# A spectral filter mixed with a Mish MLP: idle matmuls on a built-in constant, and the second piece of w1 loaded in two

## The chip, the cores and the metric

One core of one Trainium2 chip runs the whole program. The metric is the device time of one execution in microseconds, the median over several runs. The core's engines are TensorE (matmuls and transposes into PSUM), VectorE, ScalarE, GpSimd and SyncE; each works through its own queue in order, and semaphores connect them. Transfers between HBM and SBUF are issued by SyncE (SP), ScalarE or GpSimd and are carried by 16 DMA engines.

## The reference

With S = 2048 rows, D = 512 columns and F = 1792 hidden columns, all in bfloat16:

```python
def reference(A_x, A_w_r, A_w_i, B_x, B_w1, B_b1, B_w2, gate_w):
    x = A_x
    g = sigmoid((x * gate_w).sum(-1, keepdims=True))
    X = rfft2(x.astype(float32), axes=(-2, -1)) * (A_w_r + 1j * A_w_i)
    a = irfft2(X, s=(S, D), axes=(-2, -1)).astype(bfloat16)
    h = einsum("bsd,df->bsf", x, B_w1) + B_b1
    b = einsum("bsf,fd->bsd", h * tanh(softplus(h)), B_w2)
    return g * a + (1 - g) * b
```

The two branches share x. Branch a is a two-dimensional Fourier filter; branch b is a two-layer network with the Mish activation.

## The kernel before

The 2048 rows are 16 tiles of 128 rows, handled as four chunks of four tiles. The layouts keep the contraction on the 128 partitions, so each x tile is first transposed on TensorE (L516) and copied to `xT`.

Branch b: layer 1 is one group of four matmuls of 512 columns for each chunk and each of 14 hidden tiles (L575, tasks `mm1_c_ft`), Mish with the bias on ScalarE (L560), and layer 2 for each row tile (L903, the last tile in L886). For chunk 0 the first four hidden tiles are computed earlier and in finer steps, while x and w1 arrive: the tasks `early0` to `early3` take one 128-row slice of w1 each for the first half of chunk 0, and `late0` to `late3` one hidden tile each for the second half (all L590, 256 columns).

Branch a: both Fourier transforms are products with constant tables. The row transform is done per tile (`a1_t`, L609 to L612, with the table `FD`) on sums and differences of transposed tiles that VectorE forms (L541). The column transform takes two stages with a round trip through DRAM between them; the filter follows, and the inverse goes the same way back (L745 to L846). At the end the two branches are mixed and stored.

Nothing of the order is written by hand. Every piece of work is a task with an engine, a modelled duration, what it reads and writes, and a priority. `_Graph.schedule` plays the tasks through a simple model of the five engines and one DMA pipe, and the order in which it starts them becomes the order of each engine's queue. A transfer lasts its bytes divided by a rate `bw` in this model. `bw` is a number of the model alone: it changes the order in which tasks stand, never the transfer.

The head of the program, which the change touches:

- SP issues its transfers in the order in which they are written down: `ld_x00` (x tiles 0 and 2), `ld_w1d0`, `ld_x01` (tiles 1 and 3), `ld_w1d1` to `ld_w1d3` (the rest of w1's first 512 columns), `ld_w1_4` (hidden tiles 4 to 7), `ld_fd` (the table FD), `ld_x10` (chunk 1 of x), `ld_w1_8`, `ld_m1`, then the rest. `ld_b1` is issued by ScalarE. GpSimd's eight loads of the filter and two of w2 wait for `ld_w1_8`.
- VectorE fills `zt` with zeros (task `zero`, L500). ScalarE runs one Mish of one element from it (task `table`, L501), which loads the activation table.
- TensorE multiplies `zt` with itself (tasks `warm0` to `warm59`, L504) into PSUM bank 6, whose content is overwritten later. These idle matmuls are fillers: the planner takes them whenever TensorE has nothing better, and drops all that are left once `early0` has started. Of the 60, 14 remain in the program, all of 256 columns.
- `tr_small` (L519) transposes the bias; the eight transposes of x tiles 0 and 2, then of 1 and 3, are the tasks `tr0d0` to `tr1d3` (L516), and VectorE and ScalarE copy them to `xT` in turn (L529).

The lines of the idle matmuls:

```python
G.add("zero", "dve", 0.15, lambda e: e.memset(zt[:, :], 0.0), writes=["zt"], prio=99.0)
for i in range(NWARM):
    n_ = 256 if i < 15 else 128
    G.add(f"warm{i}", "pe", n_ / 1200, lambda e, n_=n_: e.matmul(ps[:, 6, 0:n_], zt[:, 0:128], zt[:, 0:n_], start=True, stop=True),
       reads=["zt"], prio=1.0).filler = True
```

Of the kernel before, what the change touches and what calls it, by code (L numbers as in the profile page):

```python
# [7 lines left out]
BF = mybir.dt.bfloat16  # L8
F32 = mybir.dt.float32
AF = mybir.ActivationFunctionType  # L10
# [305 lines left out]
def _build(nc, A_x, A_w_r, A_w_i, B_x, B_w1, B_b1, B_w2, gate_w, out):  # L316
# [9 lines left out]
    G = _Graph()  # L326
    es = ExitStack()
    with es:
        def sb(name, shape, dt):
            return es.enter_context(nc.sbuf_tensor(name, shape, dt))  # L330

        xo = sb("xo", [128, NT, 512], BF)
# [4 lines left out]
        act = sb("act", [128, 3, NFT, 512], BF)  # L337
        w1_sb = sb("w1_sb", [128, 4, F], BF)
# [8 lines left out]
        Ybuf = sb("Ybuf", [128, 32 * KR], BF)  # L347
        junk = sb("junk", [128, 512], BF)
        gwb = sb("gwb", [128, 512], BF)
        zt = sb("zt", [128, 256], BF)  # L350
        braw = sb("braw", [14, 128], BF)
        b1f = sb("b1f", [128, NFT], F32)
        gdot = sb("gdot", [128, NT], F32)
# [12 lines left out]
        q1 = sb("q1", [128, 2, 2, 16], F32)  # L366
# [25 lines left out]
        ps = es.enter_context(nc.psum_tensor("ps", [128, 8, 512], F32))  # L392
        psb = ps.bitcast(BF)

        xv = A_x[0].rearrange("(s p b) d -> p s b d", s=2, b=8)
        ov = out[0].rearrange("(s p b) d -> p s b d", s=2, b=8)
        w1v = B_w1.rearrange("(dt p) f -> p dt f", p=128)
# [7 lines left out]
        def new_sem(name):  # L405
            return es.enter_context(nc.semaphore(name))
# [5 lines left out]
        def dma(name, dst, src, reads=(), writes=(), nbytes=0, deps=(), is_out=False, prio=None, queue="sp", bw=300e3):  # L412
            dur = 1.0 if queue == "pool" else 0.5

            def fn(e, _dst=dst, _src=src):
                return e.dma_start(_dst, _src)

            t = G.add(name, queue, dur, fn, reads=reads, writes=writes, lat=2.0 + nbytes / bw, deps=deps, prio=prio)
            t.xfer = nbytes / bw
            t.isdma = True  # L420
            if is_out:
                t.sem = out_sem
                n_out_dma[0] += 1
                t.semval = 16 * n_out_dma[0]
            else:
                t.sem = new_sem("d_" + name)
                t.semval = 16
            return t
# [16 lines left out]
        def evict(name, n, dst, src, reads, writes, prio=None, rate=1.0):  # L445
# [9 lines left out]
              reads=["ones"], writes=["perm"])  # L455
        G.add("id14", "pool", 0.2, lambda e: e.affine_select(out=id14[:, :], in_=id14[:, :], pattern=[[1, 14]],
                                                             compare_op=ALU.is_equal, fill=0.0, base=0, channel_multiplier=-1),
              reads=["ones"], writes=["id14"])

        def ld_x(c, s0, s1):  # L460
            dma(f"ld_x{c}{s0}", xo[:, 4 * c + 2 * s0:4 * c + 2 * s1, :].rearrange("p (s b) d -> p s b d", b=2), xv[:, s0:s1, 2 * c:2 * c + 2, :],
                writes=[("x", t) for t in range(4 * c + 2 * s0, 4 * c + 2 * s1)], nbytes=128 * 2048 * (s1 - s0), bw=330e3 if c == 1 else 380e3)

        def ld_x0(b):
            dma(f"ld_x0{b}", xo[:, b:4:2, :], xv[:, :, b, :], writes=[("x", b), ("x", 2 + b)], nbytes=128 * 2048, bw=(218e3, 350e3)[b])

        def ld_w1d(dt_):
            dma(f"ld_w1d{dt_}", w1_sb[:, dt_, 0:512], w1v[:, dt_, 0:512], writes=[("w1d", dt_)], nbytes=128 * 1024, bw=350e3)

        def ld_w1(lo, hi):  # L470
            return dma(f"ld_w1_{lo}", w1_sb[:, :, 128 * lo:128 * hi], w1v[:, :, 128 * lo:128 * hi],
                       writes=[("w1", f) for f in range(lo, hi)], nbytes=512 * 256 * (hi - lo), bw=220e3 if lo == 4 else 380e3)

        dma("ld_b1", braw[:, :], B_b1.rearrange("(ft p) -> ft p", p=128), writes=["braw"], nbytes=3584, queue="act", prio=100.0)
        ld_x0(0)
# [1 line left out]
        ld_x0(1)  # L477
        for dt_ in range(1, 4):
            ld_w1d(dt_)
        ld_w1(4, 8)  # L480
        dma("ld_fd", FDs[:], d_FD[:], writes=["FD"], nbytes=128 * 1536, bw=262e3)
        ld_x(1, 0, 2)
        t_w1 = ld_w1(8, 14)
        dma("ld_m1", m1g1[:, 0:2048], d_M1.rearrange("p b h c m -> p (b h c m)"), writes=["m1"], nbytes=128 * 4096)
        ld_x(2, 0, 2)
# [4 lines left out]
        for i in range(2):  # L490
            for q in (0, 2, 1, 3):
                dma(f"ld_W{i}{q}", WT[32 * q:32 * q + 32, i, :, :].rearrange("p g k -> p (g k)"), Wv[i][q],
                    writes=[("W", i, q)], nbytes=32 * 8224, queue="pool", deps=[t_w1])
        WALL = [("W", i, q) for i in range(2) for q in range(4)]
        for h in range(2):
            dma(f"ld_w2_{h}", w2_sb[:, 7 * h:7 * (h + 1), :], w2v[:, 7 * h:7 * (h + 1), :],
                writes=[("w2", h)], nbytes=128 * 7 * 1024, queue="pool", deps=[t_w1])


        G.add("zero", "dve", 0.15, lambda e: e.memset(zt[:, :], 0.0), writes=["zt"], prio=99.0)  # L500
        G.add("table", "act", 1.5, lambda e: e.activation(q1[:, 0, 0, 0:1], zt[:, 0:1], AF.Mish), reads=["zt"], prio=99.0)  # L501
        for i in range(NWARM):
            n_ = 256 if i < 15 else 128
            G.add(f"warm{i}", "pe", n_ / 1200, lambda e, n_=n_: e.matmul(ps[:, 6, 0:n_], zt[:, 0:128], zt[:, 0:n_], start=True, stop=True),  # L504
               reads=["zt"], prio=1.0).filler = True


        SP0 = PR['sp0']
# [2 lines left out]
        def f_tr(e, ts, dts, at):  # L511
# [8 lines left out]
           reads=["braw", "id14"], writes=[("bank", 0)], prio=SP0 + 4.0)  # L520
        G.add("ev_small", "act", 0.25, lambda e: e.activation(b1f[:, :], psb[:, 0, 0:14], AF.Copy), reads=[("bank", 0)], writes=["b1f"], prio=SP0 + 1.05)
        for b in range(2):
            for dt_ in range(4):
                bk = (dt_ + 1) % 4
                pe(f"tr{b}d{dt_}", 2 * mm((256, 128)[b]), lambda e, dt_=dt_, bk=bk, b=b: f_tr(e, (b, 2 + b), (dt_,), lambda t, d_: (bk, t // 2)),
                   reads=[("x", b), ("x", 2 + b), "perm"], writes=[("bank", bk)], prio=SP0 + 1.0 + 2.5 * b - 0.01 * dt_)
# [3 lines left out]
                      reads=[("bank", bk)], writes=[("xT", t, dt_) for t in (b, 2 + b)], prio=SP0 + 1.1)  # L530

        for c in range(NCH):
            for t in range(4 * c, 4 * c + 4):
                if c > 0:
                    pe(f"tr{t}", 4 * mm(128), lambda e, t=t: f_tr(e, (t,), range(4), lambda t, dt_: (1, dt_)), reads=[("x", t), "perm"],
                       writes=[("bank", 1)], prio=SP0 + 1.0)
# [7 lines left out]
            for h, op in ((0, ALU.add), (1, ALU.subtract)):  # L544
# [3 lines left out]
                lo, hi = uv[:, 0:2, r2, :], uv[:, 2:4, r2, :]  # L548
# [45 lines left out]
        for dt_ in range(4):  # L594
            t_e = pe(f"early{dt_}", 4 * mm(256) * (1.8 if dt_ == 0 else 1), lambda e, dt_=dt_: f_early(e, range(4), (dt_,), 0), writes=[("bank", b) for b in EB],
                     reads=[("xT", 0, dt_), ("xT", 2, dt_), ("w1d", dt_)], prio=PR['mm1c0'] + 8)
            if dt_ == 0:
                G.filled = t_e
        for ft in range(4):
            pe(f"late{ft}", 4 * mm(256), lambda e, ft=ft: f_early(e, (ft,), range(4), 1), writes=[("bank", EB[ft])],  # L600
               reads=[("xT", t, dt_) for t in (1, 3) for dt_ in range(4)] + [("w1d", dt_) for dt_ in range(4)], prio=PR['mm1c0'] + 7 - 0.01 * ft)
            mish(0, ft, EB[ft])

        for t in range(NT):
            a1b = t % 2 if t >= 8 else 0

            def f_a1(e, t=t, a1b=a1b):
# [9 lines left out]
               writes=[("bank", a1b)], prio=SP0)  # L617
# [4 lines left out]
            if t % 4 == 3:  # L622
# [17 lines left out]
                for h in range(2):  # L640
                    t_r1w.append(dma(f"r1w{t}_{h}", scr1_w[h][:, b0:b0 + 8, :], Y1[64 * h:64 * h + 64, b0:b0 + 8, :],
                                     reads=[("Y1", b0 + i) for i in range(8)], writes=[("scr1", b0 + i, h) for i in range(8)],
                                     nbytes=64 * 8 * 512, prio=SP0 + 1.0, bw=180e3))
# [3 lines left out]
        for t in range(NT):  # L647
            G.add(f"gdot{t}", "dve", dve_dur(512) + 0.1,
                  lambda e, t=t: e.scalar_tensor_tensor(out=junk[:, :], in0=xo[:, t, :], scalar=1.0, in1=gwb[:, :],  # L649
                                                        op0=ALU.mult, op1=ALU.mult, accum_out=gdot[:, t:t + 1]),  # L650
                  reads=[("x", t), "gw"], writes=[("gd", t), "junk"], deps=s1_tasks[2:3])
# [37 lines left out]
        for n in range(4):  # L689
            t_r1r.append(dma(f"r1r{n}", In2[:, :, 2 * n:2 * n + 2, :].rearrange("p q u k -> p q (u k)"), scr1_r[:, :, 512 * n:512 * n + 512],  # L690
                             reads=[("scr1", b, h) for b in range(32) for h in range(2)],
                             writes=[("In2", q, u) for q in range(4) for u in (2 * n, 2 * n + 1)],
# [43 lines left out]
        for n in range(4):  # L736
            zb = n % 2

            def f_s2(e, n=n):
                ins = None  # L740
                for c in range(2):
                    for q in range(4):
                        for h in range(2):
# [6 lines left out]
                               reads=[("In2", q, 2 * n + uu) for q in range(4) for uu in range(2)] + ["sm"], writes=BSB))  # L750
            for i in range(4):
                h, uu = divmod(i, 2)
                u, pb = 2 * (2 * n + uu) + h, uu
                for (nm, Pb, Wu) in (("1", P1b, WT[:, :, u, 0:256]), ("2", P2b, WT[:, ::-1, u, 0:256])):
# [5 lines left out]
                          reads=[("bank", 2 * h), ("bank", 2 * h + 1)] + WALL, writes=[("P" + nm, pb)])  # L760
                for (c, nm, Pb, op) in ((0, "1", P1b, ALU.subtract), (1, "2", P2b, ALU.add)):
# [3 lines left out]
                                reads=[("P" + nm, pb)], writes=[("Z", zb, i, c)])  # L765
                if n == 0 and i == 1:
                    s2_tasks.append(pe("s2x", 0.8, f_s2x, reads=[("In2", q, u_) for q in range(4) for u_ in range(8)] + ["sm", "rr"],
                                       writes=[("bank", 0), ("bank", 1)]))
# [4 lines left out]
                          reads=["q"], writes=["zr"])  # L773
                    G.add("zi", "pool", 0.15, lambda e: e.tensor_tensor(out=zi[:], in0=q2[:, 0], in1=q2[:, 1], op=ALU.add),
                          reads=["q"], writes=["zi"])
                    G.add("z0r", "pool", 0.15, lambda e: e.tensor_tensor(out=z0[:, 0, :], in0=zr[:, 0, :], in1=zi[:, 1, :], op=ALU.subtract),
                          reads=["zr", "zi"], writes=["z0r"])
                    G.add("z0i", "pool", 0.15, lambda e: e.tensor_tensor(out=z0[:, 1, :], in0=zi[:, 0, :], in1=zr[:, 1, :], op=ALU.add),
                          reads=["zr", "zi"], writes=["z0i"])
            if n == 0:  # L780
                G.add("gexp", "pool", 2.9, lambda e: e.tensor_tensor(out=gexp[:, :], in0=gbase[:, :], in1=gdot[:, :], op=ALU.pow),  # L781
                      reads=[("gd", t) for t in range(NT)] + ["gbase"], writes=["gexp"])
                G.add("gden", "pool", 0.2, lambda e: e.tensor_scalar(out=gexp[:, :], in0=gexp[:, :], scalar1=1.0, scalar2=None, op0=ALU.add),
                      reads=["gexp"], writes=["gden"])
                G.add("gcol", "dve", 0.2, lambda e: e.reciprocal(out=gcol[:, :], in_=gexp[:, :]), reads=["gden"], writes=["gcol"])
                G.add("omg", "dve", 0.1, lambda e: e.tensor_scalar(out=omg[:, :], in0=gcol[:, :], scalar1=-1.0, scalar2=1.0, op0=ALU.mult, op1=ALU.add),
                      reads=["gcol"], writes=["omg"])
            G.add(f"wc_{n}", "pool", 0.2, lambda e, n=n, zb=zb: e.tensor_copy(
                out=Zb[:, zb, :, :, :, 0], in_=z0[:].rearrange("p c (u h) -> p h c u", h=2)[:, :, :, 2 * n:2 * n + 2]),
                reads=["z0r", "z0i"], writes=[("Z", zb, 4)])  # L790

            def f_s2i(e, zb=zb):
# [10 lines left out]
               writes=BSB)  # L803
# [3 lines left out]
            for h in range(2):  # L807
                t_r2w.append(dma(f"r2w{n}{h}", scr2_w[h][:, :, 512 * n:512 * n + 512],
                                 T2s[64 * h:64 * h + 64, :, 2 * n:2 * n + 2, :].rearrange("p q u k -> p q (u k)"),
                                 reads=[("T2s", n, 0), ("T2s", n, 1)], writes=[("scr2", n, h)], nbytes=64 * 4096))  # L810
# [3 lines left out]
        for tq in range(8):  # L814
            b0 = 4 * tq
            dma(f"r2r{tq}", T2r[:, b0:b0 + 4, :], scr2_r[:, b0:b0 + 4, :],
                reads=[("scr2", n, h) for n in range(4) for h in range(2)], writes=[("T2r", b0 + i) for i in range(4)],
# [49 lines left out]
        for c in range(NCH):  # L867
# [7 lines left out]
            for tl in range(4):  # L875
                t = 4 * c + tl
                bank = 4 + (t % 2)
                if t == NT - 1:
                    G.cur_prio = PR['mm2'] - 10
                    for i, (c0, w_) in enumerate(((0, 384), (384, 128))):  # L880
                        cs_, bk = slice(c0, c0 + w_), 1 + i

                        def f_mm2h(e, t=t, tl=tl, bk=bk, hb=hb, cs_=cs_, w_=w_):
                            ins = None
                            for ft in range(NFT):
# [5 lines left out]
                           writes=[("bank", bk)])  # L891
                        G.add(f"fin_{t}_{i}", "dve", dve_dur(w_, True),
                              lambda e, t=t, bk=bk, cs_=cs_, w_=w_: e.scalar_tensor_tensor(out=xo[:, t, cs_], in0=ps[:, bk, 0:w_], scalar=omg[:, t:t + 1],
                                                                                    in1=ga[:, t, cs_], op0=ALU.mult, op1=ALU.add),
                              reads=[("bank", bk), "omg", ("ga", t, 0), ("ga", t, 1), ("x", t)], writes=[("o", t, i)], prio=PR['fin'])
# [3 lines left out]
                for lo, hi in ((0, 4), (4, 7), (7, 11), (11, 14)):  # L899
                    def f_mm2(e, t=t, tl=tl, bank=bank, lo=lo, hi=hi, hb=hb):  # L900
# [7 lines left out]
                       reads=[("act", hb, ft) for ft in range(lo, hi)] + [("w2", lo // 7)], writes=[("bank", bank)])  # L908
                if t < NBF:
                    evict_b(t, bank)  # L910
                else:
                    G.add(f"fin_{t}", "dve", dve_dur(512, True),
                          lambda e, t=t, bank=bank: e.scalar_tensor_tensor(out=xo[:, t, :], in0=ps[:, bank, :], scalar=omg[:, t:t + 1],
                                                                           in1=ga[:, t, :], op0=ALU.mult, op1=ALU.add),
                          reads=[("bank", bank), "omg", ("ga", t, 0), ("ga", t, 1)], writes=[("x", t), ("o", t)], prio=PR['fin'])
# [116 lines left out]
```

## Time and profile before

| what | value |
|---|---|
| time, median of 3 runs (lowest, highest) | 135.4 us (135.06, 135.48) |
| the profiled execution, its time and its span | 135.63 us, 133.9 us |
| TensorE busy | 128.9 us |
| VectorE, ScalarE, GpSimd busy | 88.9, 79.6, 27.4 us |
| HBM read and written | 14.35 MB, 6.29 MB |
| `ld_x00`: issued at, to landing | 0.80 us, 2.7 us |
| `ld_w1d0`: issued at, to landing | 1.31 us, 3.4 us |
| `ld_w1_4`: issued at, to landing | 3.74 us, 5.8 us |
| `ld_fd`: issued at, to landing | 4.21 us, 5.8 us |

The span runs from the first to the last recorded instruction; the time of an execution is 1.7 us longer than its span. "Busy" is the union of an engine's recorded instructions. Matmuls overlap in their pipeline and their ends are modelled, so for TensorE the step from one start to the next tells more than the length of one.

### The profile page before, as it was taken

The numbers are of one execution on the slowest core, as the hardware profiler recorded it, in microseconds if no ns is written. First come the engines' busy times: TensorE is split into PE (matmuls) and PEld (weight loads), VectorE is DVE, ScalarE is ACT, GpSimd is POOL, SyncE is SP. The second block draws the span as 40 slices with busy tenths as digits, with TensorE's granted clock in tenths as the row PEclk, the third lists the DMA queues.
The fourth block names the chain that finished last, engine by engine and source line by source line (L and its number), as shares of the span: only waits on it lengthen the run. The fifth ranks groups of instructions, "written<-read, shape, count | busy, mean of one in ns | idle before, by whom it ended". The sixth has DMA issues, their size and how long they took to land.

```text
span 133.9 us, 2695 instructions
## 1 busy us (share of the span) xinstructions
PE 128.9 (96%) x1030; PEld 69.5 (52%) x1047; DVE 88.9 (66%) x213; ACT 79.6 (59%) x130; POOL 27.4 (20%) x56
## 2 busy tenths in 40 slices
PE   6999999999999999999999999999999999999992
PEld 4885655655544443443443443443445877755452
DVE  0286298989689982963893893794001699999422
ACT  4258798899988786605256657434333789792000
POOL 2000793014000009583440440440000000000000
PEclk9999999999999999999999999999999999999999
DMA  3899999999262399450600600600649700305321
GB/s 114 238 294 367 397 284 299 288 366 344 62 157 58 99 293 334 98 220 0 157 5 0 157 2 0 156 6 0 157 150 277 204 2 0 130 32 215 113 102 42
DMA packets 18937, 20.82 MB, mean 155 GB/s; under 512 B 1196, under 2 KB 16172, under 8 KB 18540
## 3 DMA queue, kind: packets, MB, share of 16 engines
q1 hardware_dynamic: 17888, 16.67, 41.1%
q0 software_dynamic: 864, 3.94, 9.4%
q8 instruction: 8, 0.13, 0.4%
q10 hardware_dynamic: 172, 0.04, 0.1%
q14 instruction: 5, 0.04, 0.1%
HBM read 14.35 MB, written 6.29 MB: 154 GB/s over the span
## 4 chain that ended last, share of the span: by engine, by line
PE 90%; ACT 6%; issue 1%; DVE 0%
PE ps L903 34%; PE ps L575 31%; PE ps L846 5%; ACT act L560 3%; PE ps L828 3%; ACT Ybuf L447 3%; PE ps L504 2%; PE ps L516 2%; PE ps L886 2%; PE ps L612 2%; PE ps L590 2%; PE ps L798 2%; PE ps L745 2%; PE ps L630 1%; PE ps L609 1%
## 5 line engine op out<-in xcount | busy, mean ns | idle before, releaser
L575 PE MATMUL ps<-xT,w_sb 128*128 128x512 bf16 x199 | 48.1, 379 | 0.8 <-issue 0.2
L903 PE MATMUL ps<-w_sb,act 128*128 128x512 bf16 x202 | 46.9, 379 | 0.6 <-issue 0.3
L560 ACT ACTIVATE act<-ps,b1f 128x512 bf16<-128x512 f32 x56 | 37.8, 692 | 12.8 <-PE ps L575 10.9
L903 PEld LDWEIGHTS ps<-w_sb,act 128*128 128x128 bf16 x210 | 20.2, 98 | 23.2 <-issue 1.2
L575 PEld LDWEIGHTS ps<-xT,w_sb 128*128 128x128 bf16 x208 | 19.4, 98 | 22.3 <-issue 2.1
L756 DVE TENSOR_TENSOR misc<-ps,WT 128x512 f32<-128x512 f32 x32 | 19.8, 681 | 5.9 <-PE ps L745 5.9
L858 ACT ACTIVATE xo<-ps,omg 128x512 bf16<-128x512 f32 x12 | 8.3, 690 | 19.5 <-PE ps L903 18.9
L762 POOL TENSOR_TENSOR misc<-misc 128x255 bf16<-128x255 f32 x17 | 12.1, 732 | 18.4 <-DVE misc L756 18.4
L446 DVE CAST Ybuf<-ps 128x512 bf16<-128x512 f32 (+1 forms) x9 | 8.2, 926 | 9.1 <-PE ps L798 7.3
L850 ACT ACTIVATE misc<-ps,gcol 128x512 f32<-128x512 f32 x16 | 10.7, 692 | 2.5 <-PE ps L846 2.4
L853 DVE TENSOR_TENSOR Tg<-misc 128x256 bf16<-128x256 f32 x32 | 11.7, 419 | 0.6 <-ACT misc L850 0.5
L446 DVE CAST misc<-ps 128x512 bf16<-128x512 f32 x7 | 4.8, 687 | 10.5 <-PE ps L828 10.5
L447 ACT ACTIVATE Ybuf<-ps 128x512 bf16<-128x512 f32 (+1 forms) x15 | 9.9, 714 | 2.9 <-PE ps L798 2.8
L649 DVE SCALAR_TENSOR_TENSOR junk<-xo,gwb 128x512 bf16<-128x512 bf16 x16 | 11.0, 690 | 0.7
L846 PE MATMUL ps<-GDs,misc 128*128 128x256 bf16 x64 | 9.3, 273 | 0.0
L447 ACT ACTIVATE Abuf<-ps 128x512 bf16<-128x512 f32 x13 | 7.7, 604 | 0.0
L446 DVE COPY xT<-ps 128x512 bf16<-128x512 bf16 x10 | 4.2, 422 | 4.6 <-PE ps L516 4.5
L516 PEld LDWEIGHTS ps<-pid,xo 128*128 128x128 bf16 x64 | 5.6, 111 | 3.1 <-DVE xT L446 0.4
L846 PEld LDWEIGHTS ps<-GDs,misc 128*128 128x128 bf16 x64 | 6.0, 98 | 2.1
L516 PE MATMUL ps<-pid,xo 128*128 128x128 bf16 x64 | 6.8, 243 | 0.0
L781 POOL TENSOR_TENSOR gexp<-gbase,gdot 128x16 f32<-128x16 f32 x1 | 2.9, 2943 | 18.5 <-DVE junk L649 18.5
L612 PE MATMUL ps<-FDs,Tg 128*128 128x256 bf16 x32 | 6.0, 273 | 0.0
(85 smaller groups left out, 112.8 us busy)
## 6 DMA issues: line engine op xcount, KB each, us to landing
scr<-Ybuf SPq DMA_DIRECT2D x16, 256.0 KB, 3.9
Abuf<-scr SPq DMA_DIRECT2D x4, 512.0 KB, 5.8
Abuf<-scr SPq DMA_DIRECT2D x8, 256.0 KB, 4.9
w_sb<-in_B_w_dram POOLq DMA_DIRECT2D x2, 896.0 KB, 14.2
out_dram<-xo SPq DMA_DIRECT2D x7, 256.0 KB, 2.1
xo<-in_A_x_dram SPq DMA_DIRECT2D x3, 512.0 KB, 9.8
WT<-in_A_w_r_dram POOLq DMA_DIRECT2D x4, 257.0 KB, 9.1
WT<-in_A_w_i_dram POOLq DMA_DIRECT2D x4, 257.0 KB, 10.8
```

Of the source, the lines that this page charges most:

```text
L446: G.add_multi(name, [("dve", dve_dur(n, rate=rate), lambda e: e.tensor_copy(out=dst, in_=src)), ("act", act_dur(n), lambda e: e.activation ...
L447: ("act", act_dur(n), lambda e: e.activation(dst, src, AF.Copy))],
L516: ins = e.transpose(psb[:, bank, 128 * col:128 * col + 128], xo[:, t, 128 * dt_:128 * (dt_ + 1)], perm[:, :])
L560: lambda e: e.activation(act[:, c % 3, ft, :].rearrange("p (t a b) -> p t a b", t=4, b=4), ps[:, bank, :].rearrange("p (t b a) -> p t a b" ...
L575: ins = e.matmul(ps[:, bank, :], w1_sb[:, dt_, 128 * ft:128 * (ft + 1)], xT[:, dt_, 4 * c:4 * c + 4, :], start=(dt_ == 0), stop=(dt_ == 3))
L649: lambda e, t=t: e.scalar_tensor_tensor(out=junk[:, :], in0=xo[:, t, :], scalar=1.0, in1=gwb[:, :], op0=ALU.mult, op1=ALU.mult, accum_out= ...
L756: lambda e, Pb=Pb, Wu=Wu, h=h, uu=uu, pb=pb: e.tensor_tensor(out=Pb[:, pb, :].rearrange("p (c j m) -> p c j m", c=2, j=2), in0=ps[:, 2 * h ...
L762: fz = (lambda e, c=c, Pb=Pb, op=op, pb=pb, h=h, uu=uu, zb=zb: e.tensor_tensor(out=Zb[:, zb, h, c, uu, 1:256], in0=Pb[:, pb, 1:256], in1=P ...
L846: ins = e.matmul(ps[:, yk, 256 * (j // 2):256 * (j // 2) + 256], TT[:, ts_, j // 2, s1, j % 2, :], GDs[:, j, :], start=(j % 2 == 0), stop= ...
L850: G.add(f"geo_{t}", "act", act_dur(512, True), lambda e: e.activation(gEO[:, gb, :], ps[:, yk, :], AF.Copy, scale=gcol[:, t:t + 1]), reads ...
L853: fg = (lambda e, i=i, op=op: e.tensor_tensor(out=ga[:, t, 256 * i:256 * i + 256], in0=gEO[:, gb, 0:256], in1=gEO[:, gb, 256:512], op=op))
L903: ins = e.matmul(ps[:, bank, :], act[:, hb, ft, 128 * tl:128 * (tl + 1)], w2_sb[:, ft, :], start=(ft == 0), stop=(ft == NFT - 1))
```

## The change

It does four things.

1. The tile `zt` and its zero fill go. The idle matmuls and the one-element Mish read the program's built-in constant 1.0, which is filled before the engines are released. It is one float32 number on each partition, read again and again with a step of zero. Neither waits for anything.
2. Of the idle matmuls only the first 8 have 256 columns, the others 128. The planner now keeps 17: 8 of 256 and 4 of 128 ahead of `tr_small`, 5 of 128 behind it, all ahead of the first transposes of x.
3. `ld_w1_4` is split into `ld_w1_4` (hidden tiles 4 and 5) and `ld_w1_6` (6 and 7), with `ld_fd` between them.
4. The rates of several loads in the planner's model are set anew.

```diff
-            dma(..., bw=330e3 if c == 1 else 380e3)                    # ld_x
+            dma(..., bw=308e3 if c == 1 else 380e3)
-            dma(f"ld_x0{b}", ..., bw=(218e3, 350e3)[b])
+            dma(f"ld_x0{b}", ..., bw=(403e3, 262e3)[b])
-            dma(f"ld_w1d{dt_}", ..., bw=350e3)
+            dma(f"ld_w1d{dt_}", ..., bw=(187e3, 238e3, 291e3, 187e3)[dt_])
-                       ..., bw=220e3 if lo == 4 else 380e3)            # ld_w1
+                       ..., bw={4: 194e3, 6: 291e3}.get(lo, 380e3))
-        ld_w1(4, 8)
+        ld_w1(4, 6)
         dma("ld_fd", FDs[:], d_FD[:], writes=["FD"], nbytes=128 * 1536, bw=262e3)
+        ld_w1(6, 8)
-        G.add("zero", "dve", 0.15, lambda e: e.memset(zt[:, :], 0.0), writes=["zt"], prio=99.0)
-        G.add("table", "act", 1.5, lambda e: e.activation(q1[:, 0, 0, 0:1], zt[:, 0:1], AF.Mish), reads=["zt"], prio=99.0)
+        ones = nc.const_aps.tensor(1.0, (128, 256))
+        G.add("table", "act", 1.5, lambda e: e.activation(q1[:, 0, 0, 0:1], ones[:, 0:1], AF.Mish), prio=99.0)
         for i in range(NWARM):
-            n_ = 256 if i < 15 else 128
-            G.add(f"warm{i}", "pe", n_ / 1200, lambda e, n_=n_: e.matmul(ps[:, 6, 0:n_], zt[:, 0:128], zt[:, 0:n_], start=True, stop=True),
-               reads=["zt"], prio=1.0).filler = True
+            n_ = 256 if i < 8 else 128
+            G.add(f"warm{i}", "pe", n_ / 1200, lambda e, n_=n_: e.matmul(ps[:, 6, 0:n_], ones[:, 0:128], ones[:, 0:n_], start=True, stop=True),
+                  prio=1.0).filler = True
```

In the queues that follow from it, one group moves on TensorE: the row transform of tile 0 (`a1_0`) now stands ahead of the first layer-1 group of 512 columns (`mm1_0_4`) instead of behind it, and the later transforms of chunk 0 each move up by one group. On ScalarE the evictions of these transforms move up among the Mish instructions in the same way. VectorE loses the zero fill, SP gains one transfer. The order of all else is as before.

## The prediction

> **What bounds the kernel now.** I began with the busy shares and the chain of waits on the profile's page, to find the engine whose time is the kernel's time.
>
> ```profile
> PE 128.9 (96%) x1030; PEld 69.5 (52%) x1047; DVE 88.9 (66%) x213; ACT 79.6 (59%) x130; POOL 27.4 (20%) x56
> ...
> PE 90%; ACT 6%; issue 1%; DVE 0%
> ```
>
> TensorE is busy for 128.9 of 133.9 us, and 90% of the chain that ended last is its work. Next, the list of what TensorE itself waited for:
>
> ```profile
> PE ps L504 <- DVE zt L500: 1.1, 1, 1.1
> PE ps L903 <- issue: 0.3, 2, 0.2
> PE ps L575 <- issue: 0.2, 1, 0.2
> PE ps L575 <- ACT act L560: 0.2, 1, 0.2
> ```
>
> After its first instruction TensorE waits 0.7 us in all. So whatever starts TensorE's real work later or earlier moves the end by nearly as much: nothing behind the head can swallow a delay. Third, the head in order of time, TensorE alone (start, length, line, operation, operands, count):
>
> ```profile
> 1.11 2.10 PE L504 MATMUL ps<-zt 128*128 128x256 bf16 x9 [1.11 <-DVE zt L500]
> 3.15 0.19 PE L519 MATMUL ps<-pid,braw 14*128 14x14 bf16 x1
> 3.27 1.25 PE L504 MATMUL ps<-zt 128*128 128x256 bf16 x5
> 4.31 1.06 PE L516 MATMUL ps<-pid,xo 128*128 128x128 bf16 x8
> 5.16 1.06 PE L590 MATMUL ps<-xT,w_sb 128*128 128x256 bf16 x4
> 6.01 1.06 PE L516 MATMUL ps<-pid,xo 128*128 128x128 bf16 x8
> 6.87 3.40 PE L590 MATMUL ps<-xT,w_sb 128*128 128x256 bf16 x28
> 10.31 0.81 PE L575 MATMUL ps<-xT,w_sb 128*128 128x512 bf16 x3
> ```
>
> The 14 idle matmuls (L504) stand in TensorE's queue ahead of the first transposes of x (L516). The first x piece was issued at 0.80 and landed 2.7 us later, at 3.5, so the transposes at 4.31 already wait for idle matmuls, not for data. Last, the length of one matmul of 256 columns, minimum/median/maximum in ns:
>
> ```profile
> L504 PE MATMUL ps<-zt x14: 393/421/421, 1.1 to 4.1; 128*128 128x256 bf16 x14
> ...
> L590 PE MATMUL ps<-xT,w_sb x32: 272/273/421, 5.2 to 10.0; 128*128 128x256 bf16 x32
> ```
>
> The same shape takes 421 ns early and 272 later, though the page's row of granted clock shows full speed throughout. From start to start it is 0.21 us early ((2.10-0.42)/8) and 0.109 later (ten in 1.25 us from 9.01: (1.25-0.27)/9). Single instructions put the step at 7.26. So TensorE runs at half pace for 6.15 us from its first matmul (2.95 us from its first with real data).
>
> **The change part by part.** *Idle matmuls.* Removed: the zero fill on VectorE (0.17 us) and the wait for it. TensorE can start when the engines are released, about 0.95 instead of 1.11 (VectorE's first instruction stands at 0.89). In place of 14 matmuls of 256 bf16 columns come 8 of 256 and 9 of 128, all before the first transpose, eight sources of 256 and four of 128 ahead of the bias transpose (L519). Counted as 256-column units that is 12.5 against 14, so by count alone it is a saving. But the built-in constant has type float32, and both operands are now float32. Two things follow.
>
> First, the built program holds 1067 weight loads against the 1047 of the page's first row. Three more matmuls in the source make 20 more, so each float32 matmul is laid out as two pairs of load and matmul (34 instead of 14). That makes 25 units.
>
> Second, the stream is twice as wide. No float32 matmul is in this trace. At the low end a float32 column costs what a bf16 one does (25 units); at the high end twice as much (50). The nearest rows for element width are VectorE's:
>
> ```profile
> L756 DVE TENSOR_TENSOR misc<-ps,WT 128x512 f32<-128x512 f32 x32 | 19.8, 681 | 5.9 <-PE ps L745 5.9
> L853 DVE TENSOR_TENSOR Tg<-misc 128x256 bf16<-128x256 f32 x32 | 11.7, 419 | 0.6 <-ACT misc L850 0.5
> ...
> L541 DVE TENSOR_TENSOR uv<-xT 128x1024 bf16<-128x1024 bf16 x8 | 5.5, 689 | 0.5 <-ACT xT L529 0.4
> ...
> L541 DVE TENSOR_TENSOR yb<-uv 128x512 bf16<-128x512 bf16 x8 | 3.4, 428 | 0.3
> ```
>
> Float32 costs (681-419)/256 = 1.02 ns per element, bf16 (689-428)/512 = 0.51: exactly half the rate. I take that for TensorE too: 50 units. (The Trainium skill, FP8 and Floating Point Precision, TensorE Precision Notes, says that true fp32 takes four passes through the array; by it the sum is the 50 units as well, and the low end falls away. No run here shows it yet.)
>
> How long they take depends on when the pace doubles. Measured from TensorE's first matmul the trace gives 6.15 us, and as a low bound 2.95, if only matmuls on real data count. It is one sample of one execution; I take 5.5, nearer the row that counts idle matmuls as work. Pace doubles at 0.95+5.5 = 6.45; by then 5.5/0.21 = 26.2 units are done, and the other 23.8 take 23.8 x 0.109 = 2.6 us: the first transpose starts at T = 9.0 instead of 4.31. With 6.15 us T is 9.4, with 2.95 us 7.8. (The Trainium skill, TensorE: Matmul & The Clock Gate, Part 1, has the clock rise after a full busy window of about 3.4 us that runs free of the kernel. By it the pace would double 3.4 to 6.8 us after the start, T lies between 8.0 and 9.7, and every execution has its own; the row's 6.15 lies inside.)
>
> *What the delay gives back.* At T all head transfers have landed (the slowest, the fourth early w1 piece, was issued at 3.26 and took 4.3: 7.56) and the pace is full. From T: first pair of transposes and its VectorE copy (0.29, ends at 0.60), early matmuls from 0.70, four of 0.109; eight transposes until 1.6, held by the copies (ScalarE's 0.39 each); 28 early and late matmuls x 0.109 = 3.05, until 4.64; the first transform a1_0, now ahead of mm1_0_4, 0.33; mm1_0_4, 4 x 0.215 = 0.86. The next mm1 starts at T+5.83. Before, after the same work, it started at 11.29. The delay is 9.0+5.83-11.29 = 3.6 us (3.9 with 6.15; 2.4 with 2.95).
>
> *Float32 weight loads.* At most twice the 0.15 us of a slow bf16 load, 0.09 more than a 128-column pass (0.21) for 18 passes: 1.6 us. At least nothing: the transposes step by 0.107 under loads of 0.15. I take nothing, the end that shows it on this engine.
>
> *Moves.* a1_0 goes ahead of mm1_0_4; its inputs take 1.8 us on VectorE after the last copy (before: 7.61 to 9.41), ready at T+4.3, wanted at T+4.64: nothing. On ScalarE its eviction (0.59) now stands between mish 3 and 4; mm1_0_6 needs the bank that mish 5 frees at T+7.1 and comes up at T+7.25: nothing, with 0.15 us to spare. The bias transpose comes later, behind it the bias copy and ScalarE's copies of xT; all wait for T anyway.
>
> *w1's second piece in two.* One more SP issue (0.45 us) ahead of the next x piece and all behind it; rows of 512 instead of 1024 bytes. The next x piece landed at 4.76+7.0 = 11.76 and was wanted at 11.94. If the small rows halve the rate of these 512 KB (2 us at 260 GB/s) it lands at 14 to 14.3. It is wanted at T+7.0 = 16, so 3.6 us of late TensorE hide it; without that cover it would cost up to 2.3. Later loads gain the same cover. The changed rates only steer the planner.
>
> *Sum.* -0.16 (start) is inside T; 3.6 us pass through. The profiled execution took 135.63 (span 133.9 and 1.7 around it), 0.23 above the median of 135.4. 135.63+3.6 = 139.2 for it; for the median **139.0**.
>
> **The rivals.** *Two cheap passes:* 25 units, all at half pace, T = 0.95+25 x 0.21 = 6.2, delay 0.8 to 0.9: 136.3. For it: the layout shows two instructions, not four. Against it: VectorE's rows.
>
> *The pace never doubles under idle matmuls:* constant data may not count as activity (the pace rose 2.95 us after the first real data). 50 units cold, T = 11.45, then the old head's pace, 6.98 us from first transpose to second mm1: 11.45+6.98-11.29 = 7.1, 142.5. Against it: idle matmuls on zeros would then have been worth nothing.
>
> *Not slower:* the pace doubles one step sooner because the earlier start and denser stream fill the activity count by 3.9, and float32 costs two passes. 14 units cold, 11 x 0.109 = 1.2: T = 5.1. It decides from T below 11.29-5.83 = 5.46. The early matmuls then wait for the w1 piece at 7.56: 7.6+20 x 0.109+0.33+0.86 = 11.0, 0.3 us ahead: 135.1. For it: the saving in columns and the dropped wait. Against it: it needs both cheap passes and an early rise; with 50 units an early rise still leaves T at 7.8.
>
> **How the numbers follow.** Forecast 0.81, cheap passes 0.07, no doubling 0.06, not slower 0.06. The forecast's own span is 2.4 to 3.9, plus loads up to 1.6: 137.8 to 140.9. I set 137.2 to 140.4, which leaves the rivals and a little of the forecast's upper edge out. A measurement tells 0.3% (0.4 us) from no change; 135.1 lies inside that, so of the 0.06 I give 0.03 to faster, 0.04 to same with a little of the cheap passes, and 0.93 to slower.
>
> **What would show it.** Right: L504 as about 34 float32 matmuls in the trace, the last near 9 us, steps of about 0.42 us for 256 columns at first and 0.21 later; the first L516 at 8 to 9.7; then 28 L590 at 0.109 without a wait; from the second L575 on, every row of before 2.4 to 4 us later. Wrong: the first L516 before 6, or TensorE waits behind the head that shrink by a microsecond or more.

## The result, and the profile after

The changed kernel takes 139.22 us (median of 6 runs, 138.25 to 139.59), the kernel before 135.43 us on the same chip. The ratio is 1.0275, with a 95% interval of 1.0238 to 1.0311: 2.75% slower, some 3.8 us. The profiled execution took 139.59 us, with a span of 137.9.

The busy shares and the chain of waits on the page of the changed kernel:

```profile
PE 134.5 (98%) x1067; PEld 73.5 (53%) x1067; DVE 88.6 (64%) x212; ACT 79.4 (58%) x130; POOL 27.1 (20%) x56
...
PE 95%; ACT 3%; DVE 0%; issue 0%
PE ps L903 33%; PE ps L575 32%; PE ps L504 6%; PE ps L846 5%; PE ps L590 3%; PE ps L828 3%; PE ps L886 2%; PE ps L612 2%; PE ps L516 2%; PE ps L798 2%; PE ps L745 2%; PE ps L630 1%; ACT Ybuf L446 1%; ACT act L560 1%; PE ps L609 1%; PE ps L610 1%
```

TensorE is still the kernel's time. L504, the idle matmuls, has grown from 2% to 6% of the chain. In order of time (start, length, what) the chain shows them, and the last group of matmuls, as follows, first in the kernel before and then in the changed one:

```profile
1.11 2.10 PE ps L504 x9
3.33 1.18 PE ps L504 x5
...
128.39 3.07 PE ps L886 x28
```

```profile
0.83 7.34 PE ps L504 x24
8.29 1.31 PE ps L504 x10
...
132.38 3.07 PE ps L886 x28
```

The idle matmuls now stand on the path that sets the end with some 8.7 us; before they had 3.3 us. The head of TensorE in order of time shows where the difference arises (start, length, line, operation, operands, count):

```profile
0.83 7.34 PE L504 MATMUL ps<-const-float32-1.0 128*128 128x256 f32 x24 [0.83 <-PEq L1017]
8.11 0.18 PE L519 MATMUL ps<-pid,braw 14*128 14x14 bf16 x1
8.22 1.38 PE L504 MATMUL ps<-const-float32-1.0 128*128 128x128 f32 x10
9.44 0.61 PE L516 MATMUL ps<-pid,xo 128*128 128x128 bf16 x8
10.10 0.61 PE L590 MATMUL ps<-xT,w_sb 128*128 128x256 bf16 x4
10.54 0.61 PE L516 MATMUL ps<-pid,xo 128*128 128x128 bf16 x8
10.99 3.22 PE L590 MATMUL ps<-xT,w_sb 128*128 128x256 bf16 x28
14.05 0.22 PE L609 MATMUL ps<-FDs,Tg 128*128 128x128 bf16 x1
...
14.38 1.03 PE L575 MATMUL ps<-xT,w_sb 128*128 128x512 bf16 x4
15.32 0.23 PE L609 MATMUL ps<-FDs,Tg 128*128 128x128 bf16 x1
...
15.66 1.03 PE L575 MATMUL ps<-xT,w_sb 128*128 128x512 bf16 x4
```

The 17 idle matmuls of the source are 34 in the trace. The first row mixes 16 of 256 columns and 8 of 128 (the shape printed is that of one). Early on the 256-column ones step by 0.427 us (2.25, 2.67, 3.10, 3.53 are starts in a row), twice the 0.21 us of a bfloat16 one before; from 6.47 on they step by 0.22. The first transpose of x stands at 9.44 instead of 4.31, though its data landed at 3.8. From there the head runs tighter than before, because everything has landed and the pace is full: the work that ended at 11.29 now ends at 15.32, 4.03 us later. At the other end of the kernel the last group of matmuls (L886) starts at 132.38 instead of 128.39, 3.99 us later. Next to nothing in between was given back.

The form of the idle matmuls' rows, minimum/median/maximum in ns, and all that TensorE waited for in the whole execution:

```profile
L504 PEld LDWEIGHTS ps<-const-float32-1.0 x34: 185/190/337, 0.8 to 9.2; 128*128 128x128 f32 x34
L504 PE MATMUL ps<-const-float32-1.0 x34: 272/326/766, 0.8 to 9.3; 128*128 128x128 f32 x18, 128*128 128x256 f32 x16
...
PE ps L504 <- PEq L1017: 0.8, 1, 0.8
```

In this trace all 1067 matmuls are recorded, and after its start TensorE waits for nothing. The four waits behind the head, 0.7 us together, that the prediction read from the trace before stand at gaps in that record: 17 matmuls are missing there (1030 of 1047), and the traces of these experiments show the same 0.7 us where matmuls are missing and none of it where all are there.

### The profile page after: what moved, and what is told of

The parts are those of the page before. It is cut to its first block, busy times and chain, and to the rows that moved or that the text cites. A ratio compares the mean times of both kernels' runs of the same rounds, so it can differ in the third digit from the quotient of the medians.

```text
span 137.9 us, 2755 instructions
## 1 busy us (share of the span) xinstructions
PE 134.5 (98%) x1067; PEld 73.5 (53%) x1067; DVE 88.6 (64%) x212; ACT 79.4 (58%) x130; POOL 27.1 (20%) x56
## 4 chain that ended last, share of the span: by engine, by line
PE 95%; ACT 3%; DVE 0%; issue 0%
PE ps L903 33%; PE ps L575 32%; PE ps L504 6%; PE ps L846 5%; PE ps L590 3%; PE ps L828 3%; PE ps L886 2%; PE ps L612 2%; PE ps L516 2%; PE ps L798 2%; PE ps L745 2%; PE ps L630 1%; ACT Ybuf L446 1%; ACT act L560 1%; PE ps L609 1%; PE ps L610 1%
## 5 line engine op out<-in xcount | busy, mean ns | idle before, releaser
L575 PE MATMUL ps<-xT,w_sb 128*128 128x512 bf16 x208 | 49.6, 379 | 0.1
L903 PE MATMUL ps<-w_sb,act 128*128 128x512 bf16 x210 | 48.3, 379 | 0.0
L560 ACT ACTIVATE act<-ps,b1f 128x512 bf16<-128x512 f32 x56 | 38.0, 692 | 12.7 <-PE ps L575 10.8
L504 PE MATMUL ps<-const-float32-1.0 128*128 128x128 f32 (+1 forms) x34 | 8.7, 425 | 0.8 <-PEq L1017 0.8
L504 PEld LDWEIGHTS ps<-const-float32-1.0 128*128 128x128 f32 x34 | 7.2, 249 | 2.0 <-issue 0.8
L529 DVE COPY xT<-ps 128x256 bf16<-128x256 bf16 x4 | 1.0, 292 | 10.3 <-PE ps L516 10.3
```

The lines of the kernel that those rows point to most:

```text
L560: lambda e: e.activation(act[:, c % 3, ft, :].rearrange("p (t a b) -> p t a b", t=4, b=4), ps[:, bank, :].rearrange("p (t b a) -> p t a b" ...
L575: ins = e.matmul(ps[:, bank, :], w1_sb[:, dt_, 128 * ft:128 * (ft + 1)], xT[:, dt_, 4 * c:4 * c + 4, :], start=(dt_ == 0), stop=(dt_ == 3))
L903: ins = e.matmul(ps[:, bank, :], act[:, hb, ft, 128 * tl:128 * (tl + 1)], w2_sb[:, ft, :], start=(ft == 0), stop=(ft == NFT - 1))
```

## The experiments

Nine runs follow, one of them the changed kernel once more. Each comparison is with the kernel before on the same chip. The ratios are those on record and not the quotients of the two medians; the two differ by up to 0.1%.

**The type alone.** The changed kernel with the bfloat16 constant:

```diff
-        ones = nc.const_aps.tensor(1.0, (128, 256))
+        ones = nc.const_aps.tensor(1.0, (128, 256), BF)
```

> The changed kernel with one word more: the idle matmuls read the built-in bfloat16 constant 1.0 in place of the float32 one. Their number, sizes and places, all queues and all transfers are those of the changed kernel. Theory (the type alone makes the idle matmuls four times as long): they take about 12.5 units of 0.21 us, the first transpose of x starts at 3.7 to 4.0 instead of 9.44, and the delay of the head is gone. What is left is the split of w1: the next x piece landed at 5.24+7.5 = 12.7 in the changed kernel and would now be wanted at about 12, so TensorE waits 0.5 to 1.0 us for it; 135.5 to 136.4. Rival (number, place or order of the idle matmuls make the loss): 138.5 to 139.6, first transpose after 8 us. Rival (the split costs nothing): 135.0 to 135.3.

Measured: 135.83 us (135.14 to 136.72, 12 runs), before 135.44; ratio 1.0029 (1.0006 to 1.0051). One word takes back 3.4 of the 3.8 us. The head of TensorE and its waits, in the trace of this kernel:

```profile
0.84 2.29 PE L504 MATMUL ps<-const-bfloat16-1.0 128*128 128x256 bf16 x12 [0.84 <-PEq L1017]
...
3.81 0.85 PE L516 MATMUL ps<-pid,xo 128*128 128x128 bf16 x8
...
PE ps L516 <- DMA xo<-in_A_x_dram: 0.5, 1, 0.5
PE ps L590 <- DMA w_sb<-in_B_w_dram: 0.3, 1, 0.3
```

The first transpose stands at 3.81, and now TensorE waits for transfers: 0.5 us for the next x piece and 0.3 for a piece of w1. The lead of half a microsecond is not kept. The first rival falls: the number, places and order of the idle matmuls are the same here. A split without cost would have given 135.0 to 135.3; some 0.4 us remain, about as much as TensorE waits for the x piece.

**The split alone.** The kernel before with w1's second piece in two and model rates of 140e3 and 240e3 for its halves, which make the planner write the changed kernel's queues:

```diff
-        ld_w1(4, 8)
+        ld_w1(4, 6)
         dma("ld_fd", ...)
+        ld_w1(6, 8)
```

> The kernel before with w1's second piece loaded in two and the transform's table between, and model rates under which the planner gives exactly the changed kernel's queues; the idle matmuls are the 14 bfloat16 ones on zeros. Theory: the small rows make the next x piece land 1.0 us later (12.7 instead of 11.76), and with TensorE on time it is wanted at about 12.2, so 0.3 to 0.8 us are lost: 135.7 to 136.2. Rival (harmless): 135.1 to 135.5. Rival (the split makes part of the 3.8 us): 137 or more.

Measured: 135.54 us (134.90 to 136.17, 12 runs), before 135.44; ratio 0.9999 (0.9982 to 1.0017). The theory missed: no loss. The next x piece was issued at 5.25 and landed 7.1 us later, at 12.35, and was wanted at 12.41. It came 0.6 us later than before, but with the transforms moved ahead it was also wanted later: TensorE came to it at 12.16 in the kernel before. The split cost something only where TensorE came earlier, as in the experiment above.

**The float32 idle matmuls alone.** The kernel before with these and without the zero fill, and the loads, rates and other queues of before:

```diff
-NWARM = 60
+NWARM = 17
-            n_ = 256 if i < 15 else 128
+            n_ = 256 if i < 8 else 128
-            ... e.matmul(ps[:, 6, 0:n_], zt[:, 0:128], zt[:, 0:n_], ...), reads=["zt"]
+            ... e.matmul(ps[:, 6, 0:n_], ones[:, 0:128], ones[:, 0:n_], ...)
```

> The kernel before with the 17 float32 idle matmuls of the changed kernel and no zero fill; the loads, their order and all other queues are those before. Theory: the first transpose starts at 8 to 9.7 us and the whole loss is here: 138.2 to 139.6, within 0.4 us of the changed kernel. Rival (the split and the moved transform carry part of it): 137.5 or less.

Measured: 139.15 us (138.72 to 139.52, 5 runs), before 135.44; ratio 1.0272 (1.0251 to 1.0294). The whole loss, to within the intervals, without any change of the loads.

**The bfloat16 constant with the old loads.** The kernel before without the zero fill; 15 idle matmuls of 256 columns remain.

> The kernel before without the zero fill: the idle matmuls read the built-in bfloat16 constant and wait for nothing; the planner keeps 15 of 256 columns. Loads and all else as before. Theory: the start at 0.83 instead of 1.11 is filled by one idle matmul more, the first transpose starts at 4.2 to 4.4 as before: 135.2 to 135.5, no change. Rival (ones in place of zeros change when the pace doubles): a different step of the pace in the trace, and up to 0.4 us either way.

Measured: 135.30 us (135.25 to 135.83, 12 runs), before 135.44; ratio 0.9997 (0.9985 to 1.0009): no change. The first transpose stood at 4.00, 0.2 us earlier than expected; the early matmuls then waited 0.3 us for a piece of w1. The pace had doubled at 3.8 us, much earlier than the 7.2 of the kernel before, and even so no time was won. Whether the value had a part in that moment this run alone does not tell; two below bear on it.

**Fewer float32 idle matmuls.** `NWARM = 6` in the changed kernel.

> The changed kernel with 6 float32 idle matmuls of 256 columns in place of 17 (all ahead of the bias transpose, none behind it); all else as in the changed kernel. Theory (the loss is the time that the idle matmuls hold TensorE's queue): 12 half-rate passes x 0.427 = 5.1 us, so the first transpose starts at 6.2 to 6.6 if the pace stays low until then (earlier if it doubles sooner), 2.9 to 3.2 us ahead of the changed kernel; 135.8 to 136.9. Rival (any float32 idle matmul costs the head, by its type and not by its length): 138 or more.

Measured: 136.03 us (135.39 to 136.56, 10 runs), before 135.68; ratio 1.0024 (0.9998 to 1.0050). The profiled execution took 136.53 with its first transpose at 6.34; the pace doubled only then, at 6.4. It is the length of the row that costs, not the type as such.

**The changed kernel once more.**

> The changed kernel once more, unchanged. In the six profiles so far the pace doubled at 3.9, 4.3, 6.3, 6.4, 6.9 and 7.3 us, and the times of the changed kernel span 1.3 us. If the moment is drawn anew in every execution, this profile has another moment than 6.4 by some tenths or more, the first transpose starts half of that difference earlier or later than 9.44, and the time follows. If the moment belongs to the kernel (float32 passes bring it at 6.3 to 6.4), it stands there again and the first transpose at 9.3 to 9.5.

Measured: 138.43 us, one run, 1.16 us less than the profiled run above, from the same program. Its head:

```profile
0.84 6.21 PE L504 MATMUL ps<-const-float32-1.0 128*128 128x256 f32 x24 [0.84 <-PEq L1017]
6.97 0.18 PE L519 MATMUL ps<-pid,braw 14*128 14x14 bf16 x1
7.08 1.38 PE L504 MATMUL ps<-const-float32-1.0 128*128 128x128 f32 x10
8.30 0.61 PE L516 MATMUL ps<-pid,xo 128*128 128x128 bf16 x8
```

Here the pace doubled at 4.1 us (the steps go from 0.43 to 0.22 between 3.96 and 4.47) instead of 6.4. Half of that difference is 1.16 us, and the first transpose came 1.14 us earlier. The moment does not belong to the kernel alone; it differs from one execution to the next.

**Zeros in float32.** `nc.const_aps.tensor(0.0, (128, 256))` in the changed kernel.

> The changed kernel with the built-in float32 constant 0.0 in place of 1.0. Theory: the value has no part in it; 138.2 to 139.6, and the pace doubles while the idle matmuls run, 3 to 6.8 us after the first. Rival (idle matmuls on zeros do not count as activity): the pace stays low through all of them, first transpose at 11.5 to 11.9, 142 or more.

Measured: 139.02 us (138.59 to 139.72, 4 runs), before 135.68; ratio 1.0241 (1.0197 to 1.0285). The pace doubled at 5.0 us, while nothing but idle matmuls on zeros ran. Float32 constants, zeros included, count as work for the pace. That the bfloat16 zeros of the kernel before do is not shown: in the two profiles with them the pace doubled 2.9 and 2.6 us after the first transposes of x had begun.

**Four bfloat16 matmuls for each float32 one.** Each of the 17 issued four times, with the bfloat16 constant:

```diff
-            ... lambda e, n_=n_: e.matmul(ps[:, 6, 0:n_], ones[:, 0:128], ones[:, 0:n_], ...)
+            ... lambda e, n_=n_: [e.matmul(ps[:, 6, 0:n_], ones[:, 0:128], ones[:, 0:n_], ...) for _ in range(4)][-1]
```

> The changed kernel with bfloat16 idle matmuls, each issued four times (32 of 256 columns and 36 of 128 in the places of 8 and 9). Theory (a float32 matmul is worth four bfloat16 ones and nothing else of it matters): the first transpose starts at 8 to 9.9, 138.2 to 139.8, as the changed kernel. Rival (something of float32 beyond its length, such as a switch between types or its weight loads): 0.6 us or more under the changed kernel.

Measured: 139.41 us (138.78 to 139.93, 4 runs), before 135.68; ratio 1.0278 (1.0236 to 1.0319). Four times the bfloat16 passes take as long as the float32 ones. Nothing of float32 beyond its length is needed to explain the loss.

**No idle matmuls.** `NWARM = 0` in the kernel with the bfloat16 constant and the old loads.

> The kernel with the bfloat16 constant and the loads of before, with all 15 idle matmuls left out; every other queue is as there. What are idle matmuls worth, against which a too long row of them stands? Theory (the pace doubles some 3.3 to 6.5 us after TensorE begins to work, drawn anew each time; five profiles of that kind gave 3.1 to 6.2): TensorE begins at about 3.6, the pace doubles between 7 and 10, and the early and late matmuls run at half pace for up to 3 us more: 135.4 to 136.8, median near 136.0. Rival (the head is held by the transfers anyway): 135.1 to 135.5.

Measured: 135.64 us (135.20 to 136.49, 12 runs), before 135.52; ratio 1.0010 (0.9993 to 1.0028). The pace doubled at 7.3 us, as expected, but the median lies 0.4 us below the expected 136.0 and 0.1 above the rival's range. The first transpose stood at 3.79, and TensorE waited for transfers:

```profile
PE ps L518 <- DMA braw<-in_B_b_dram: 3.1, 1, 3.1
PE ps L515 <- DMA xo<-in_A_x_dram: 0.5, 1, 0.5
...
PE ps L589 <- DMA w_sb<-in_B_w_dram: 0.2, 1, 0.2
```

The idle matmuls are worth at most 0.3% in this kernel; the rival, that the transfers hold the head anyway, is nearer the median. No version here beats the kernel before by more than the measurement tells.

The profiled executions side by side, with the start of the first transpose, the moment at which the pace doubles, and the time. In nine of the traces the moment is the start of the stretch for which a full granted clock is recorded, and the steps of single instructions agree with it; e2 and e9 have no such record, and there it is read from the steps, to some 0.1 us:

```
                             pace doubles   first transpose   time     time - first transpose
e9 no idle matmuls              7.3             3.79         135.86         132.07
e1 bf16 constant                4.3             3.81         135.65         131.84
e5 bf16 constant, old loads     3.8             4.00         135.30         131.30
e2 split alone                  6.9             4.30         135.48         131.18
before                          7.2             4.31         135.63         131.32
e4 six float32                  6.4             6.34         136.53         130.19
e6 changed again                4.1             8.30         138.43         130.13
e8 four times bf16              4.8             8.63         138.78         130.15
e7 float32 zeros                5.0             8.73         138.87         130.14
e3 float32 alone                6.2             9.31         139.37         130.06
changed                         6.4             9.44         139.59         130.15
```

From 6.3 us on the time is 130.1 us plus the start of the first transpose, within 0.1 us, whatever kind of matmul held it up. Up to 4.3 us the start does not matter: the five kernels stand at 135.3 to 135.9. In e1, e5 and e9 TensorE then waits for transfers; in the kernel before and in e2 it waits for none, but its first 2.9 and 2.6 us of work on x run at the low pace. Nothing was run between 4.3 and 6.3 us; the line meets those five times at 5.2 to 5.8, which is an estimate of where the start begins to count.

## Why the prediction was right

It said 139.0, 137.2 to 140.4, slower; 139.22 was measured. By its own steps:

- *Idle matmuls as 50 units, twice by layout and twice by stream width.* Right. The trace has 34 float32 matmuls, a 256-column one steps by 0.427 us at the low pace against 0.21, and the run with four bfloat16 matmuls for each shows the factor of four as a time. That VectorE's rows have the same half rate made them a good guide, but by luck as much as by reason: nothing on record tied the one engine to the other. The Trainium skill's four passes for fp32 (FP8 and Floating Point Precision, TensorE Precision Notes) agree with these steps.
- *The pace doubles 5.5 us after the start.* It did in the profiled execution (0.83 to 6.41), but the single number is luck: in eleven profiles the moment lies anywhere from 2.9 to 6.1 us after the first matmul. The forecast's own span, 2.4 to 3.9 us of delay, was what could be known. By the Trainium skill (TensorE: Matmul & The Clock Gate, Part 1) the clock rises after a full busy window of about 3.4 us that runs free of the kernel, so 3.4 to 6.8 us after the start. The traces agree with a range about as wide as the window, but not with its lower end: 2.92 us of work (0.84 to 3.76 in the bfloat16 constant with the old loads) and 3.26 us (0.84 to 4.10 in the changed kernel once more) were enough. The stretch recorded at full clock lasts 126.29, 129.71 or 133.12 us in the nine traces, which is 37, 38 and 39 times 3.413 us. If the moments stand at the ends of windows of that length, all eleven profiles fit: windows with at most 2.7 us of work in them changed nothing, those with 2.9 us or more doubled the pace. This is inferred; no run here set the window's phase.
- *T = 9.0.* Measured 9.44, the largest error among the terms, and about the 0.4 us by which the profiled execution (139.59) missed its 139.2. The first pass took 0.56 us instead of 0.427; between the twelfth idle matmul and the thirteenth the bias transpose took about 0.2 us more than its place in a stream; both had been left out.
- *What the delay gives back, 5.83 us from T.* Measured 5.88 (9.44 to 15.32). The text named the next mm1 as the end of this stretch, but in the changed queue a1_1 comes first: a1_1 is at 15.32 and the mm1 at 15.66. The arithmetic compared the same work before and after, the name was wrong.
- *Float32 weight loads hidden.* Right: they show 0.19 us at the high pace, longer than the 0.11 us step of the 128-column passes above them there, and the steps stayed as narrow as the stream makes them. The bound for one load was too low: at most 0.30 us was allowed, 0.34 is measured at the low pace, where only 256-column passes ran.
- *Moves at no cost.* Right; the split with the moved transform alone is at 0.9999 of before.
- *The split hidden by 3.6 us of late TensorE, up to 2.3 without the cover.* Hidden, yes: the x piece landed at 12.7 and was transposed at 16.5. The bound was too wide: the piece landed 1.0 us later than before, not the 2.2 to 2.5 that halved rows would give, and without the cover TensorE waited 0.5 us for it.
- *The delay passes through in full.* Right to 0.1 us: 4.03 us at the end of the head, 3.99 at the last group.
- *The rivals.* Two cheap passes: fell by the 0.427 us steps (its own terms give a delay of 6.2+5.83-11.29 = 0.74 us, not 0.8 to 0.9; the table's line gives the same 136.3). The pace never doubles under idle matmuls: fell, on float32 ones and zeros and on bfloat16 ones. Not slower: fell with T at 9.44; its limit for T, 5.46, agrees with the table, where the line meets the early kernels between 5.2 and 5.8.

## What to carry to other kernels

Look at the type of every operand of a matmul, also where its result is thrown away: here one with two float32 operands cost four bfloat16 ones in TensorE's queue, and filler in an in-order queue delays whatever stands behind it. Count filler by its time in the queue at the low pace, and end it when the first data land; here the first 3 us were free and, from some point between 4.3 and 6.3 us on, every further microsecond cost its full length. Before tuning filler, run the kernel without any: here that cost nothing that could be measured.

## What the runs showed of the hardware that had not been expected

The moment at which TensorE's pace doubles differed between two executions of one program by 2.3 us (6.4 and 4.1), and the time of a kernel with a long head on TensorE followed it by half: 1.16 us. That is nearly the whole spread of the changed kernel, 138.25 to 139.59, against 135.06 to 135.53 for the kernel before in the same comparison; of the other executions there is no profile. The row of granted clock on the page shows none of it, because time without a clock record reads as full there; the trace's clock records, which begin at 6.41 and 4.10 us, and the steps between starts do.

Transposes follow the pace as other matmuls do: 128 columns step by 0.107 us at the low pace (the eight at 4.31 in the kernel before take 1.06 us) and by 0.056 at the high one (the eight at 9.44 in the changed kernel take 0.61).
